# Gated mix of two attentions on one core: moved rows keep their place in the transfer queue, and two subtractions trade engines

## The chip, the core and the metric

The kernel runs on one core of a Trainium2 chip. A core has TensorE (PE) for matrix products, VectorE (DVE), ScalarE (ACT) and GpSimd (POOL) for elementwise work, and SyncE (SP), which in this kernel issues every transfer (DMA). Each engine takes its instructions in order. An instruction that waits for a semaphore holds back all that stand behind it on its engine. The metric is the device time of one execution in microseconds, the median of several runs.

## The reference

The input `x` has 2048 rows of 448 numbers. Two attentions with 16 heads of 28 numbers are computed from it and mixed by a gate:

```
g = sigmoid((x * gate_w).sum(-1))
# A, linear attention with learned softmax features
pq, pk = q @ w_phi, k @ w_phi                          # per head
phi_q  = [softmax(pq), softmax(-pq)]; phi_k likewise   # 56 features a head
num    = phi_q @ (phi_k.T @ v)
den    = phi_q @ sum_rows(phi_k) + 1e-6
a      = (num / den) @ woA
# B, softmax attention
b      = softmax(q @ k.T / sqrt(28)) @ v @ woB
out    = g * a + (1 - g) * b
```

Everything is float32. Where one float32r pass is not exact enough, an operand is split into a high part and a low part (`x - high`), and the product is made of three passes.

## The kernel before

The program is written out as one long sequence. TensorE, VectorE, ScalarE and GpSimd run their instructions in the order in which the source emits them (`manual_schedule`). SyncE is not among the engines named there: a scheduler of the framework places its transfers, as far as the data allow, and a transfer may so be put ahead of or behind another that the source wrote earlier.

There are four stages. Up to about 173 us the kernel splits `x` and the weights and makes B's queries and keys and A's key features. From 173.9 us (the first `pq`) it makes A's queries, features and outputs, up to the last `poa` at 315.2 us. Then it makes the rest of B's values, and from about 340 us (`st`, `pv`, `pm`) B's attention runs to the end. All along, scan units (`mx_unit`, tiles `pmb`, `pmd`, `rl`) look for the largest score of each query in B, as VectorE's L305 and ScalarE's L303.

The change lies in A's outputs. Here the loop over `i` (L803 and after) works on 16 blocks of 128 query rows, with two blocks to a *tile*; there are tiles 0 to 7. For each tile these steps follow one another over several turns of the loop, and the steps of neighbouring tiles interleave:

- `numer` (L560 to L572): TensorE makes numerators and denominators in `pn`, from transposed features `fT` and the key sums `KV`.
- `normalize1` (L410): ScalarE copies both halves of `pn` to `oU`. A transfer gathers the denominators, which stand in every 32nd row, into `den` (L416; `dena`, "the gather").
- `normalize2` (L419): VectorE adds a small number and takes the reciprocal (L422, L423). One transfer writes it to `rd` in memory (L426; `rda`, "the inverse"), and four read it back, spread over 32 rows each, into `rs` (L431; `rsa`, "the broadcasts").
- `normalize3` (L435): VectorE multiplies `oU` by `rs` (L437).
- `normalize4` (L440): for each of the two halves `k`, ScalarE makes the high part (L444), and VectorE or GpSimd the low part (L445), in `oT`. VectorE does it for `k == 0`, GpSimd for `k == 1`.
- `take_spread` (L453): four transfers (L457; `oTa<-oTa`, "the moved rows") copy rows of one low part into rows of `oT` that are otherwise empty, which saves TensorE one pass of twelve. They need both low parts.
- `out_a`, `out_a2` (L623 to L635): eleven passes of TensorE for each block, in `poa` (so tile n serves `poa` of blocks 2n and 2n+1); ScalarE multiplies by the gate into `ga`, and a transfer stores it in `gad` (L635, "the gated store").

`normalize1` and `normalize2` are also used by B, with `n == 1` (`denb`, `rdb`, `rsb`); A calls them with `n == 2`. Behind these transfers on SyncE's queue stand others that the text names: `qp` (L185), rows of queries for the scan units, and `vb` (L917, L918), copies of three early blocks of B's values.

Of the kernel before, what the change touches and what calls it, by code (L numbers as in the profile page):

```python
# [17 lines left out]
P = 128  # L18
# [3 lines left out]
DH = 28  # L22
# [13 lines left out]
def f32(ap):  # L36
    return ap.bitcast(F32)
# [3 lines left out]
def gated_mix_kernel(ctx, tc, xT, wqkB, wvB, wvA, wkAT, wqAT, phi, woA, woB,  # L41
# [7 lines left out]
    nc = tc.nc  # L49
# [348 lines left out]
    def fold(dst, nm, g, b0=0, n=4):  # L398
# [8 lines left out]
        nc.scalar.copy(dst[:, 0, bs, gs], pw3)  # L407
        nc.vector.tensor_sub(dst[:, 1, bs, gs], pw3, f32(dst[:, 0, bs, gs]))

    def normalize1(pool, pn, nm, n):  # L410

        oU = pool.tile([P, n, 512], F32, tag="oU", name=f"oU{nm}", bufs=1 + n)
        for i in range(n):
            (nc.scalar.copy if n == 2 else nc.vector.tensor_copy)(oU[:, i, :], pn[i])
        den = pool.tile([P, 16 * n], F32, tag="den", name=f"den{nm}", bufs=2)
        nc.sync.dma_start(den, oU[DH:P:32].rearrange("p n q -> p (n q)"))  # L416
        return oU, den

    def normalize2(pool, oU, den, nm, n, eps):  # L419

        if eps:
            nc.vector.tensor_scalar_add(den, den, EPS)  # L422
        nc.vector.reciprocal(den, den)  # L423
        rd = dr.tile([4, n * 512], F32, tag=f"rd{n}", name=f"rd{nm}", bufs=2)
        rs = pool.tile([P, n, 512], F32, tag="rs", name=f"rs{nm}", bufs=2)
        nc.sync.dma_start(rd, den)  # L426
        if n == 1:
            nc.sync.dma_start(rs[:, 0, :], rd.unsqueeze(1).to_broadcast([4, 32, 512]))
            return oU, rs
        for j in range(4):  # L430
            nc.sync.dma_start(rs[32 * j:32 * j + 32].rearrange("p n q -> p (n q)"),  # L431
                              rd[j:j + 1].to_broadcast([32, n * 512]))
        return oU, rs

    def normalize3(oU, rs, n):  # L435
# [4 lines left out]
    def normalize4(pool, oU, nm, n):  # L440

        o = pool.tile([P, n, 2, 512], F32R, tag="oT", name=f"oT{nm}", bufs=2)
        for k in range(n):
            (nc.scalar.copy if n == 2 else nc.gpsimd.tensor_copy)(o[:, k, 0, :], oU[:, k, :])  # L444
            (nc.vector if n == 2 and k == 0 else nc.gpsimd).tensor_sub(  # L445
                o[:, k, 1, :], oU[:, k, :], f32(o[:, k, 0, :]))
        if n == 2:
            spread.append(o)
        return [o[:, k] for k in range(n)]
# [3 lines left out]
    def take_spread():  # L453
        while spread:
            o = f32(spread.pop())
            for r in range(0, P, 32):
                nc.sync.dma_start(  # L457
                    o[r + DH:r + 32].rearrange("p k i n -> p (k i n)")[:, :1792].rearrange(
                        "p (s n) -> p s n", n=256),
                    o[r:r + DH, 1, 1, 256:])  # L460

    def out_passes(oT, c, w, g):
        tt = slice(c, c + P)
# [96 lines left out]
    def numer(tb):  # L560

        pn = [ps_s(f"pn{tb}_{i}") for i in range(2)]
        for gp in range(2):
            for r in range(2):
                for c in range(4):
                    n, rows = 4 * gp + c, slice(64 * r, 64 * r + 56)
                    h = 2 * n + r
                    nc.tensor.matmul(pn[r][32 * c:32 * c + 32, gp * 256:gp * 256 + 256],
                                     KV[rows, 32 * h:32 * h + 32], fT_of[tb][rows, n, :],
                                     start=True, stop=True, tile_position=(64 * r, 32 * c),  # L570
                                     skip_group_check=True)
        num[tb] = normalize1(ta, pn, f"a{tb}", 2)  # L572
# [230 lines left out]
    for i in range(2 * NT + 12):  # L803
        t, q = i, i - NT
# [65 lines left out]
        if y >= 9 and y % 2 and tb - 4 < 8:  # L870
            oTs[tb - 4] = normalize4(ta, num.pop(tb - 4), f"a{tb - 4}", 2)
            take_spread()
# [48 lines left out]
        if y >= 5 and y % 2 and tb - 2 < 8:  # L921
            num[tb - 2] = normalize2(ta, *num[tb - 2], f"a{tb - 2}", 2, True)
# [258 lines left out]
    def finish(gq, s):  # L1181
# [5 lines left out]
        def f1():  # L1187
            st["n"] = normalize1(late_p, [pv_of[gq]], f"b{gq}", 1)

        def f2():  # L1190
            st["n"] = normalize2(late_p, *st["n"], f"b{gq}", 1, False)
# [4 lines left out]
        def f4():  # L1196
            st["o"], = normalize4(late_p, st["n"], f"b{gq}", 1)
            if g < NG - 1:
                for j in range(4):
                    r = (4 * g + j) * DH  # L1200
                    nc.sync.dma_start(o_d[r:r + DH, :, qb * 512:(qb + 1) * 512],
                                      f32(st["o"][32 * j:32 * j + DH]))
# [168 lines left out]
```

## Time and profile before

| what | value |
|---|---|
| median of 3 runs | 1008.03 us (1007.89 to 1008.36) |
| profiled execution | 1007.33 us, of which the span of instructions is 1005.5 us |
| granted TensorE clock, mean | 0.997 |
| TensorE busy | 993.6 us, 99% |
| ScalarE busy | 807.4 us, 80% |
| VectorE busy | 670.0 us, 67% |
| GpSimd busy | 230.8 us, 23% |
| transfers | 109.09 MB, mean 108 GB/s |

All times inside the profile are counted from the start of the span. In a row of a timeline stand the start, the length, the engine, the line of the source, the operation, what is written and read, and how many instructions were merged; brackets give the idle time of the engine before it and what ended that. An engine with a `q` behind its name is its sequencer, which waits and issues transfers: the length of such a row is the time of issuing, not that of the transfer. The length of a matmul is modelled, so neighbouring ones overlap in the list. A wait for several semaphores is put down to the one that came last by the profile, which is not always the one that counted.

### The profile page before, as it was taken

What the parts mean: (1) busy time and instruction counts of PE and PEld (TensorE: products, weight loads), DVE (VectorE), ACT (ScalarE), POOL (GpSimd) and SP (SyncE); (2) the same over time, 40 slices, a digit from 0 to 9 for tenths busy, and PEclk for the clock granted to TensorE, in tenths of its full rate; (3) what the DMA queues carried; (4) which work ended last, traced back from release to release, by engine and by line L of the source; (5) the groups of instructions that cost most, each with busy time, mean ns of one, the idle gap of its engine ahead of it and who ended that gap; (6) DMA issues with size and microseconds to landing.
All of it is one profiled execution on the core that took longest, in us unless ns stands there. A gap on an engine that the chain in (4) does not pass through costs nothing.

```text
span 1005.5 us, 18087 instructions
## 1 busy us (share of the span) xinstructions
PE 993.6 (99%) x6456; PEld 555.5 (55%) x6456; DVE 670.0 (67%) x1343; ACT 807.4 (80%) x1532; POOL 230.8 (23%) x214
## 2 busy tenths in 40 slices
PE   9999999999989999999999999999999999999998
PEld 7878878887677533333333333333334444455656
DVE  5467666889755588888888788887886444544202
ACT  5445555568755799999999999999999999979672
POOL 1265455678414311110120101102011011101010
PEclk9999999999999999999999999999999999999999
DMA  8976312411444842332624324343233264216231
GB/s 283 318 242 212 115 62 81 165 46 54 127 147 104 168 110 50 89 78 51 130 58 107 80 52 139 82 107 92 61 85 79 52 130 114 61 37 149 63 104 56
DMA packets 69170, 109.09 MB, mean 108 GB/s; under 512 B 18216, under 2 KB 29112, under 8 KB 69080
## 3 DMA queue, kind: packets, MB, share of 16 engines
q1 hardware_dynamic: 69080, 107.94, 39.7%
q8 instruction: 51, 0.84, 0.4%
q14 instruction: 39, 0.32, 0.1%
HBM read 74.33 MB, written 31.45 MB: 105 GB/s over the span
## 4 chain that ended last, share of the span: by engine, by line
PE 95%; SPq 1%; DMA 1%; DVE 1%; ACT 0%; issue 0%; POOL 0%; POOLq 0%; ACTq 0%; DVEq 0%
PE st L1036 28%; PE pv L1140 25%; PE pm L337 9%; PE pqk L118 6%; PE pva L136 4%; PE pk L136 4%; PE pq L118 4%; PE pob L118 3%; PE pvb L136 2%; PE poa L118 2%; PE pmb L296 2%; PE pft L554 1%; PE pqk L721 1%; PE pkv L508 1%; PE poL L1178 1%; SPq L457 1%
## 5 line engine op out<-in xcount | busy, mean ns | idle before, releaser
L1039 ACT ACTIVATE p<-st 128x512 f32<-128x512 f32 x1020 | 527.8, 642 | 25.7 <-PE st L1036 25.7
L348 DVE TENSOR_REDUCE part<-pm 128x1 f32<-128x512 f32 x450 | 287.5, 685 | 150.5 <-PE pm L337 150.5
L1036 PE MATMUL st<-qst,kst 128*128 128x512 f32 x1020 | 301.1, 423 | 0.3 <-DVE acc L1155 0.3
L1140 PE MATMUL pv<-p,vb 128*32 128x512 f32 x2048 | 263.6, 602 | 0.0
L1036 PEld LDWEIGHTS st<-qst,kst 128*128 128x128 f32 x1020 | 168.7, 187 | 99.5 <-ACT p L1039 45.0
L341 ACT ACTIVATE rl<-pm 128x512 f32<-128x512 f32 x200 | 124.7, 624 | 14.0 <-PE pm L337 13.1
L337 PEld LDWEIGHTS pm<-kc,qc 28*128 28x128 f32 x800 | 38.2, 181 | 167.7 <-issue 100.6
L437 POOL TENSOR_TENSOR oUb<-oUb,rsb 128x512 f32<-128x512 f32 x15 | 19.4, 1291 | 458.2 <-DMA rsb<-rdb 293.4
L345 DVE CUSTOM_DVE_ANT_0 rl<-pm,rl 128x512 f32<-128x512 f32 x150 | 102.1, 681 | 0.0
L337 PE MATMUL pm<-kc,qc 28*128 28x512 f32 x800 | 101.1, 495 | 0.0
L1140 PEld LDWEIGHTS pv<-p,vb 128*32 128x32 f32 x2048 | 47.4, 108 | 95.6 <-issue 88.9
L305 DVE CUSTOM_DVE_ANT_0 rl<-pmb,rl 128x512 f32<-128x512 f32 x112 | 72.0, 681 | 36.8 <-ACT rl L303 36.8
L303 ACT ACTIVATE rl<-pmd 128x1024 f32<-128x1024 f32 x56 | 57.5, 1028 | 17.7 <-issue 8.7
L118 PE MATMUL pqk<-XH,wB 128*128 128x512 f32 x192 | 59.3, 397 | 0.0
L658 ACT CAST ev<-pqk 128x512 fp32r<-128x512 f32 x28 | 16.1, 588 | 38.0 <-PE pqk L118 29.7
L118 PE MATMUL poa<-woA_s,oTa 128*128 128x448 f32 x128 | 39.2, 388 | 6.5 <-DMA oTa<-oTa 3.7
L118 PEld LDWEIGHTS pqk<-XH,wB 128*128 128x128 f32 x192 | 35.4, 188 | 8.5 <-issue 1.5
L1155 DVE SCALAR_TENSOR_TENSOR acc<-pob,gate,acc 128x448 f32<-128x448 f32 x12 | 8.2, 680 | 47.2 <-PE pob L118 47.2
L136 PE MATMUL pva<-wvA_s,XH 128*128 128x450 f32 x128 | 38.6, 375 | 0.0
L659 DVE TENSOR_TENSOR ev<-pqk,ev 128x512 fp32r<-128x512 f32 x28 | 19.0, 690 | 27.8 <-ACT ev L658 27.7
L136 PE MATMUL pk<-wkA_s,XH 128*128 128x448 f32 x128 | 37.4, 373 | 0.0
L118 PE MATMUL pq<-wqA_s,XH 128*128 128x448 f32 x128 | 37.3, 374 | 0.0
(169 smaller groups left out, 1177.7 us busy)
## 6 DMA issues: line engine op xcount, KB each, us to landing
qkd<-ev SPq DMA_DIRECT2D x28, 512.0 KB
qst<-qkd SPq DMA_DIRECT2D x64, 224.0 KB
kst<-qkd SPq DMA_DIRECT2D x64, 224.0 KB
od<-oTb SPq DMA_DIRECT2D x48, 112.0 KB
rsa<-rda SPq DMA_DIRECT2D x32, 128.0 KB
rsb<-rdb SPq DMA_DIRECT2D x15, 256.0 KB
kc<-qkd SPq DMA_DIRECT2D x64, 56.0 KB
gad<-ga SPq DMA_DIRECT2D x16, 224.0 KB
```

Of the source, the lines that this page charges most:

```text
L118: nc.tensor.matmul(d, l, r, start=i == 0, stop=i == len(todo) - 1)
L136: nc.tensor.matmul(dst[:, :n], l, r, start=i == 0, stop=i == len(todo) - 1, skip_group_check=True)
L296: nc.tensor.matmul((pb if j < 2 else pd)[:, j % 2, :], qc[js, qt * P:(qt + 1) * P], kc[js, :], start=True, stop=True, tile_position=(32 * ...
L303: nc.scalar.activation(rl, pd, AF.Relu)
L305: nc.vector.tensor_tensor_reduce(rl[:, i, :], pb[:, i, :], rl[:, i, :], 1.0, LOWEST, ALU.add, ALU.max, part[:, col + i:col + i + 1])
L337: nc.tensor.matmul(pm[j], mxs[("qc", gq)][js, qt * P:(qt + 1) * P], mxs[("kc", g, kb)][js, :], start=True, stop=True, tile_position=(32 * ...
L341: nc.scalar.activation(rl, pm[kb], AF.Relu if kb < 3 else AF.Copy)
L345: nc.vector.tensor_tensor_reduce(r, pm[j], r, 1.0, LOWEST, ALU.add, ALU.max, part[:, col + j:col + j + 1])
L348: nc.vector.tensor_reduce(part[:, col + j:col + j + 1], pm[j], AX.X, ALU.max)
L1036: nc.tensor.matmul(st, kst_of[(gq // NQ, kt // 4)][:, j, (kt % 4) * P:(kt % 4 + 1) * P], qst_of[gq][:, j, :], start=True, stop=True)
L1039: nc.scalar.activation(p, st, AF.Exp, scale=SCALE)
L1140: nc.tensor.matmul(pv[32 * j:32 * j + 32, :], vb[kt // 8][:, kt % 8, 4 * g + j, :], pt[j], start=kt == 0, stop=kt == NT - 1, tile_position ...
```

## The change

The 32 transfers of moved rows, the 32 broadcasts, the 8 gathers and the 8 inverses of A get a common token. Transfers that carry one token keep the order in which the source emits them, among themselves; the scheduler still places all others. The same transfers of B (`n == 1`) get none. The gated stores get none either and stay on SyncE. In `normalize4` VectorE now makes the low part of the second half (`k == 1`) and GpSimd that of the first. No instruction is added or removed; the rows of TensorE, VectorE, ScalarE and GpSimd stand in the same order as before.

```diff
+    def kept(x, n=2):
+        if n == 2:
+            tc.stamp_issue_order_token(x.ins, "turns")
+
     def normalize1(pool, pn, nm, n):
...
-        nc.sync.dma_start(den, oU[DH:P:32].rearrange("p n q -> p (n q)"))
+        kept(nc.sync.dma_start(den, oU[DH:P:32].rearrange("p n q -> p (n q)")), n)
...
-        nc.sync.dma_start(rd, den)
+        kept(nc.sync.dma_start(rd, den), n)
...
         for j in range(4):
-            nc.sync.dma_start(rs[32 * j:32 * j + 32].rearrange("p n q -> p (n q)"),
-                              rd[j:j + 1].to_broadcast([32, n * 512]))
+            kept(nc.sync.dma_start(rs[32 * j:32 * j + 32].rearrange("p n q -> p (n q)"),
+                                   rd[j:j + 1].to_broadcast([32, n * 512])))
...
-            (nc.vector if n == 2 and k == 0 else nc.gpsimd).tensor_sub(
+            (nc.vector if n == 2 and k == 1 else nc.gpsimd).tensor_sub(
                 o[:, k, 1, :], oU[:, k, :], f32(o[:, k, 0, :]))
...
             for r in range(0, P, 32):
-                nc.sync.dma_start(
+                kept(nc.sync.dma_start(
                     o[r + DH:r + 32].rearrange("p k i n -> p (k i n)")[:, :1792].rearrange(
                         "p (s n) -> p s n", n=256),
-                    o[r:r + DH, 1, 1, 256:])
+                    o[r:r + DH, 1, 1, 256:]))
```

What this does to SyncE's queue is seen at two places. The first is around the moved rows of tiles 2 and 3. The digit behind `dena`, `rda` and `rsa` is the tile, as that behind `oTa`; the digit behind `ga` is the block. Line numbers of the changed kernel are 4 higher here. Before:

```order
L635 DMA gad0_69<-ga0_2687 128x448
L426 DMA rda3_2692<-dena3_2599 128x32
L416 DMA dena4_2749<-oUa4_2746 128x1x32
L635 DMA gad0_69<-ga1_2769 128x448
L457 DMA oTa2_2814<-oTa2_2814 4x7x256
L431 DMA rsa3_2693<-rda3_2692 32x1024 x4
L457 DMA oTa2_2814<-oTa2_2814 4x7x256 x3
L635 DMA gad0_69<-ga2_2852 128x448
L426 DMA rda4_2857<-dena4_2749 128x32
L416 DMA dena5_2917<-oUa5_2914 128x1x32
```

The same stretch of SyncE's queue in the changed kernel:

```order
L639 DMA gad0_69<-ga0_2687 128x448
L430 DMA rda3_2692<-dena3_2599 128x32
L639 DMA gad0_69<-ga1_2769 128x448
L185 DMA qp3_0_3141<-qkd_68 28x512 x2
L435 DMA rsa3_2693<-rda3_2692 32x1024 x4
L420 DMA dena4_2749<-oUa4_2746 128x1x32
L461 DMA oTa2_2814<-oTa2_2814 4x7x256 x4
L639 DMA gad0_69<-ga2_2852 128x448
L430 DMA rda4_2857<-dena4_2749 128x32
L639 DMA gad0_69<-ga3_2937 128x448
```

The broadcasts of the next tile moved from the middle of the moved rows to a place ahead of all four, the gather of the tile after it moved behind those broadcasts, and two loads of `qp` came ahead of them. The second place is the end of the stage, tiles 5 to 7, on SyncE's queue before:

```order
L416 DMA dena7_3177<-oUa7_3174 128x1x32
L635 DMA gad1_70<-ga7_3192 128x448
L457 DMA oTa5_3218<-oTa5_3218 4x7x256 x4
L635 DMA gad2_71<-ga8_3239 128x448
L426 DMA rda7_3257<-dena7_3177 128x32
L635 DMA gad2_71<-ga9_3291 128x448
L457 DMA oTa6_3304<-oTa6_3304 4x7x256
L431 DMA rsa7_3258<-rda7_3257 32x1024 x4
L457 DMA oTa6_3304<-oTa6_3304 4x7x256 x3
L635 DMA gad2_71<-ga10_3325 128x448
L917 DMA vb0_3129<-ve0_2060 128x1024
```

And the same stretch of SyncE's queue in the changed kernel:

```order
L639 DMA gad1_70<-ga7_3192 128x448
L435 DMA rsa6_3135<-rda6_3134 32x1024 x4
L420 DMA dena7_3177<-oUa7_3174 128x1x32
L461 DMA oTa5_3218<-oTa5_3218 4x7x256 x4
L639 DMA gad2_71<-ga8_3239 128x448
L430 DMA rda7_3257<-dena7_3177 128x32
L639 DMA gad2_71<-ga9_3291 128x448
L921 DMA vb0_3129<-ve0_2060 128x1024
L435 DMA rsa7_3258<-rda7_3257 32x1024 x4
L461 DMA oTa6_3304<-oTa6_3304 4x7x256 x4
L639 DMA gad2_71<-ga10_3325 128x448
```

Here the gated store of block 7 moved ahead of the broadcasts of tile 6, and the larger `vb` copy ahead of those of tile 7, which no longer part the moved rows of tile 6.

## The prediction

> **What bounds the kernel now.** I read the page's busy table and the chain that ended last first, then a table of three stretches, then the list of what TensorE waited for. In the rows of a stretch, the first pair is its length and TensorE's busy time; the granted clock stands third from the end.
>
> ```profile
> PE 993.6 (99%) x6456; PEld 555.5 (55%) x6456; DVE 670.0 (67%) x1343; ACT 807.4 (80%) x1532; POOL 230.8 (23%) x214
> ...
> PE 95%; SPq 1%; DMA 1%; DVE 1%; ACT 0%; issue 0%; POOL 0%; POOLq 0%; ACTq 0%; DVEq 0%
> ...
> 230.00:325.00 95.00, 88.53 (x581) 68.76 (x580) 63.93 (x136) 60.76 (x95) 40.18 (x33) 0.98 0.37 110
> 325.00:950.00 625.00, 624.65 (x3839) 265.52 (x3837) 435.79 (x883) 589.07 (x1173) 72.72 (x67) 1.00 0.38 89
> ...
> PE poa L118 <- DMA oTa<-oTa: 3.7, 2, 2.4
> PE poa L118 <- DMA gad<-ga: 1.9, 1, 1.9
> ...
> PE poa L118 <- ACT rl L303: 0.6, 2, 0.4
> ...
> PE poa L118 <- ACT vb L790: 0.3, 1, 0.3
> ```
>
> TensorE is the bound: 99% busy, 95% of the chain. It stands idle 11.9 us in all (1005.5 minus 993.6), and 6.5 us of that (95.00 minus 88.53) lie between 230 and 325 us, where A's output is made: the stage that the change touches. All its waits there are ahead of `poa`, the output projection of A. From 325 to 950 it waits 0.35 us in all, so an earlier start of that stretch should arrive whole at the end. The five waits by name, from TensorE's timeline, with two pieces of the chain and the clock in one of them:
>
> ```profile
> 257.02 0.64 PE L118 MATMUL poa<-woA_s,oTa 128*128 128x448 f32 x2 [0.40 <-ACT rl L303]
> ...
> 267.65 0.64 PE L118 MATMUL poa<-woA_s,oTa 128*128 128x448 f32 x2 [1.93 <-DMA gad<-ga]
> ...
> 276.99 0.65 PE L118 MATMUL poa<-woA_s,oTa 128*128 128x448 f32 x2 [0.29 <-ACT vb L790]
> ...
> 287.39 1.09 PE L118 MATMUL poa<-woA_s,oTa 128*128 128x448 f32 x2 [2.36 <-DMA oTa<-oTa]
> ...
> 310.26 0.64 PE L118 MATMUL poa<-woA_s,oTa 128*128 128x448 f32 x2 [1.31 <-DMA oTa<-oTa]
> ...
> 287.39 3.88 PE poa L118 x11
> ...
> 310.26 2.48 PE poa L118 x11
> ...
> 287.40:291.10 3.70, 3.70 (x11) 3.34 (x12) 1.70 (x3) 0.00 (x0) 1.22 (x3) 0.59 0.06 21
> ```
>
> These are the first matmuls of tiles 2, 3, 4, 5 and 7 (`oTa2` to `oTa7`). Now SyncE's own queue at the same places, which issues in order; oTa are the moved rows (L457), rsa the broadcasts (L431):
>
> ```profile
> 226.91 2.74 SPq L457 DMA_DIRECT2D oTa<-oTa  x4
> ...
> 252.18 1.98 SPq L457 DMA_DIRECT2D oTa<-oTa  x3
> ...
> 259.93 0.64 SPq L457 DMA_DIRECT2D oTa<-oTa  x1
> 260.67 2.07 SPq L431 DMA_DIRECT2D rsa<-rda  x4
> 262.78 1.98 SPq L457 DMA_DIRECT2D oTa<-oTa  x3
> ...
> 272.17 1.98 SPq L457 DMA_DIRECT2D oTa<-oTa  x3
> ...
> 281.14 0.42 SPq L635 DMA_DIRECT2D gad<-ga  x1
> 281.69 2.98 SPq L457 DMA_DIRECT2D oTa<-oTa  x4
> ...
> 304.50 2.79 SPq L457 DMA_DIRECT2D oTa<-oTa  x4
> ```
>
> From the end of the last moved row to the matmul: 254.16 to 257.02, 264.76 to 267.65, 274.15 to 276.99, 284.67 to 287.39, 307.29 to 310.26. That is 2.86, 2.89, 2.84, 2.72 and 2.97 us: one constant, the landing. So all five waits are for moved rows, also the three where the list names ScalarE or a gated store, and each ends earlier by as much as the last moved row is issued earlier. In tile 3 the first row goes at 259.93, four broadcasts of the next tile come between, and the other three follow.
>
> **The change, part by part.** *The token* puts the four moved rows together, and each tile's broadcasts ahead of them, so the broadcasts go while the queue still waits for the low parts. Unbroken, four rows take 2.74 us (tile 0). In tile 3 the span from first to last, 259.93 to 264.76, is 4.83, so 2.09 us go. Tiles 2 and 4 have the same break.
>
> - Tile 2: the 0.40 wait is smaller than that and goes: gain 0.40.
> - Tile 3: 1.93 minus 2.09, plus 0.40 by which TensorE now arrives earlier, leaves 0.24: gain 1.69.
> - Tile 4: 0.29 goes: gain 0.29. Its multiplication (L437, below) also waited 2.54 us for a broadcast that stood behind moved rows; that goes too.
> - Tile 5: its rows were not broken up, but late in the queue, and their subtractions are late:
>
> ```profile
> 277.72 1.13 ACT L444 CAST oTa<-oUa 128x512 fp32r<-128x512 f32 x2
> ...
> 278.93 1.30 POOL L445 TENSOR_TENSOR oTa<-oUa,oTa 128x512 fp32r<-128x512 f32 x1 [8.49 <-ACT oTa L444]
> ...
> 279.08 1.69 DVE L445 TENSOR_TENSOR oTa<-oUa,oTa 128x512 fp32r<-128x512 f32 x1
> ...
> 267.74 0.69 DVE L445 TENSOR_TENSOR oTa<-oUa,oTa 128x512 fp32r<-128x512 f32 x1
> ...
> 302.61 1.28 POOL L445 TENSOR_TENSOR oTa<-oUa,oTa 128x512 fp32r<-128x512 f32 x1 [13.98 <-ACT oTa L444]
> ...
> 302.71 1.73 DVE L445 TENSOR_TENSOR oTa<-oUa,oTa 128x512 fp32r<-128x512 f32 x1
> ```
>
> *The swap of the low parts.* VectorE's subtraction takes 0.69 alone (267.74) and 1.69 or 1.73 when GpSimd's runs: it ends 0.54 after GpSimd's (280.77 against 280.23), so the two go one after the other. GpSimd had the second half and waited for both casts (to 278.85). Now it has the first and may start after one cast, about half of 1.13 earlier; VectorE, busy with a scan until 279.08, still ends 0.54 behind it. So the pair ends 0.55 earlier in tiles 5 and 7. In tiles 0 to 3, where GpSimd is busy with features, I take nothing for it: its bounds there are 0 and 0.57.
>
> Tile 5 then: low parts at 280.2, and the queue is free, where it issued a store at 281.14 and the first row at 281.69. That is 1.44 earlier. TensorE arrives 0.29 earlier relative to the casts (the wait of tile 4 lies between). Wait: 2.36 plus 0.29 minus 1.44 is 1.21: gain 1.15. After this wait alone the clock fell: 0.59, and eleven matmuls took 3.88 against 2.48 after the 1.31 wait. The 1.93 wait had no such loss, so a wait of 1.21 should have none: gain 1.40. The Trainium skill ("TensorE: Matmul & The Clock Gate", Part 1) has the clock fall after an idle window of about 3.4 us. By that rule 2.36 us would not do it, the cause would be another, and the sum would be 1.40 less; the trace shows the fall right behind the gap, and I go by it.
>
> - Tile 7: GpSimd waited for both casts here too (13.98 <-ACT), and the rows went at once after VectorE (304.44 to 304.50), so only the swap counts, 0.55 to 0.60: gain 0.60 of 1.31.
>
> Sum: 0.40 + 1.69 + 0.29 + 1.15 + 1.40 + 0.60 = 5.5 us.
>
> **What is moved behind.** The gather of the next tile (`dena`, L416) now stands behind the broadcasts, and its reciprocal has a fixed place on VectorE. In tile 4 two `qp` loads stand ahead of the broadcasts, and the first waits for the scan unit's matmul at 244.39:
>
> ```profile
> 244.39 0.50 PE L296 MATMUL pmd<-kp,qp 28*128 28x512 f32 x2
> ...
> 249.74 0.12 DVE L422 TENSOR_SCALAR dena<-dena 128x32 f32<-128x32 f32 x1
> ...
> 250.99 0.62 DVE L472 TENSOR_REDUCE extq<-pcq 128x16 f32<-128x448 f32 x1 [0.74 <-ACT pcq L470]
> ...
> 265.38 1.23 DVE L437 TENSOR_TENSOR oUa<-oUa,rsa 128x1024 f32<-128x1024 f32 x1 [2.54 <-DMA rsa<-rda]
> ...
> 280.46 0.58 SPq L416 DMA_DIRECT2D dena<-oUa  x1
> ...
> 282.50 0.18 DVE L422 TENSOR_SCALAR dena<-dena 128x32 f32<-128x32 f32 x1 [1.73 <-DMA dena<-oUa]
> ...
> 274.74 2.57 DMA rda<-dena
> ...
> 250.75 1.09 PE L568 MATMUL pn<-fT,KV 56*32 56x256 f32 x32
> ...
> 259.86 1.09 PE L568 MATMUL pn<-fT,KV 56*32 56x256 f32 x32
> ```
>
> Tile 4: matmul done 244.9; two loads 0.8 (a 0.4 issue each, by `gad`'s 0.42); four broadcasts 2.07; gather 0.58; landing 1.46 (281.04 to 282.50): 249.8, against 249.74 in the place on VectorE, where 0.74 of idle follows. So it costs nothing, by a hair; from -0.5 (the 2.54 wait gone) to 0.7 for a slip are its bounds. A turn of the queue is now serial: gather 0.58, landing 1.46, reciprocal 0.5, inverse 2.57, broadcasts 2.07: 7.2 us, against 9.1 between the closest numerators (250.75 to 259.86). One half-megabyte copy (`vb`) now goes ahead of the last broadcasts; tile 6 had no wait, and I take none. The gated stores keep their engine and stand earlier or where they stood.
>
> **The rivals.**
> 1. *Part only*: tile 7 and 5 gain nothing by the swap, because the scan or the queue keeps them, and the clock still falls. Then 0.40 + 1.69 + 0.29, and 0.60 in tile 5 (1.15 less 0.55): 3.0, so 1005.0. For: VectorE's order is unchanged. Against: 8.49 and 13.98 us of idle GpSimd.
> 2. *The clock's loss stays*, its cause being something else than the gap: 5.5 minus 1.4 gives 1003.9. For: the 1.93 gap, nearly as long, had none. Against: it begins at the longest gap and nowhere else. The rule of the Trainium skill on the clock gate, above, is on this rival's side.
> 3. *The gather's turn becomes the bound*: late gathers hold VectorE at L422, and with it features and transposes. It decides once a turn exceeds 9.1 us; 7.2 plus two loads and a late store leaves about 1 us. At 2.6 over, in three tiles, it costs 7.8 against 5.5: 1010.3, slower.
> 4. *Hidden*: the waits move to another place in the stage, or the order differs without effect: 1008.0.
>
> **How the numbers follow.** The profiled execution took 1007.33 (span 1005.5 and 1.8 around it), 0.7 under the median of 1008.03. The sum gives 1001.8 against it and 1002.5 against the median, which I predict. All five waits and the clock's loss gone would be 7.7: 1000.3, the low end. 0.2%, about what can be told from no change, is 2.0 us: 1006.0, the high end, which takes in rivals 1 and 2. Chances: forecast 0.55, rival 1 0.17, rival 2 0.08, rival 3 0.11, rival 4 0.07, below the range 0.02. So faster 0.82, same 0.07, slower 0.11, and the range holds 0.80.
>
> **What would show it.** Four moved rows in one piece in every tile; waits of `poa` near 0, 0.2, 0, 1.2 and 0.7 us; clock 1.00 all through 280 to 300; GpSimd's L445 about 0.5 ahead in tiles 5 and 7; the 2.54 wait of L437 gone. I am wrong if L422 shows waits that TensorE feels, if the wait in tile 6 appears behind the `vb` copy, or if the stretch from 325 on is entered earlier and yet ends at the old time.

## The result and the profile after

The changed kernel takes 1001.9 us (median of 6 runs, 1001.0 to 1002.38), the kernel before 1007.96 (6 runs, 1007.44 to 1008.36): a ratio of 0.9939 with a 95% interval of 0.9926 to 0.9952. Forecast were 1002.5 us. The profiled execution took 1001.51 us, its span is 999.7. Line numbers are 4 higher than before. The page's busy row, two rows of the table of stretches and the list of TensorE's waits, all of the changed kernel:

```profile
PE 991.4 (99%) x6456; PEld 553.5 (55%) x6456; DVE 666.3 (67%) x1343; ACT 807.4 (81%) x1532; POOL 231.7 (23%) x214
...
230.00:325.00 95.00, 92.07 (x606) 71.26 (x606) 62.68 (x144) 62.97 (x97) 46.01 (x36) 1.00 0.44 121
325.00:950.00 625.00, 624.63 (x3840) 264.61 (x3840) 433.94 (x877) 590.48 (x1178) 66.90 (x63) 1.00 0.37 88
...
PE poa L118 <- DMA oTa<-oTa: 2.4, 3, 1.3
PE poa L118 <- ACT vb L794: 0.2, 1, 0.2
PE poa L118 <- ACT rl L303: 0.2, 1, 0.2
```

TensorE's idle time between 230 and 325 us fell from 6.5 to 2.9 us (95.00 minus 92.07), and the clock there is 1.00 instead of 0.98. From the end of the last `poa` to the end of the span it is 689.9 us before and 690.0 after, so the gain arrived whole. TensorE's timeline at the first `poa` of tiles 3, 4, 5 and 7 (tile 2 waits no more), the piece of the chain behind the longest wait, and SyncE's moved rows of tiles 2, 3, 5 and 7:

```profile
264.83 0.65 PE L118 MATMUL poa<-woA_s,oTa 128*128 128x448 f32 x2 [0.39 <-DMA oTa<-oTa]
...
274.10 0.65 PE L118 MATMUL poa<-woA_s,oTa 128*128 128x448 f32 x2 [0.22 <-ACT vb L794]
...
283.45 0.65 PE L118 MATMUL poa<-woA_s,oTa 128*128 128x448 f32 x2 [1.31 <-DMA oTa<-oTa]
...
304.40 0.64 PE L118 MATMUL poa<-woA_s,oTa 128*128 128x448 f32 x2 [0.75 <-DMA oTa<-oTa]
...
283.45 2.48 PE poa L118 x11
...
248.41 2.64 SPq L461 DMA_DIRECT2D oTa<-oTa  x4
...
259.18 2.63 SPq L461 DMA_DIRECT2D oTa<-oTa  x4
...
277.72 2.65 SPq L461 DMA_DIRECT2D oTa<-oTa  x4
...
298.66 2.68 SPq L461 DMA_DIRECT2D oTa<-oTa  x4
```

The rows go in one piece everywhere. Waits of 0, 0.39, 0.22, 1.31 and 0.75 us stand where 0.40, 1.93, 0.29, 2.36 and 1.31 stood, and the eleven matmuls after the wait in tile 5 take 2.48 instead of 3.88 us.

One part of the difference is not the change's. The spans differ by 5.8 us: 3.6 in waits of `poa`, 1.4 in the clock, and 0.9 already ahead of the first `poa` (232.73 before, 231.80 after). TensorE's timeline shows where, at the very start, of before:

```profile
1.36 3.79 PE L704 MATMUL pqk<-ident 128*128 128x128 f32 x16 [1.36 <-POOL ident masks.py:199]
5.09 3.04 PE L721 MATMUL pqk<-XH,wB 128*128 128x512 f32 x8
```

and of the changed kernel:

```profile
1.36 3.68 PE L708 MATMUL pqk<-ident 128*128 128x128 f32 x16 [1.36 <-POOL ident masks.py:199]
4.86 2.06 PE L725 MATMUL pqk<-XH,wB 128*128 128x512 f32 x8
```

The same eight matmuls took 3.04 and 2.06 us. The clock's record has its first change at 7.15 us before and at 4.80 after, and over the thirteen profiles of this study that moment lies between 4.35 and 7.57 us, and the first `poa` between 231.34 and 232.87 us, later by 0.46 us for each us. So a single profile carries up to 1.5 us of chance from its start. For the experiments I therefore also give *the stage*, the time from the first `poa` to the end of the last: 82.9 us before, 77.9 after, 5.0 less. A stage is that of one profile, and its own chance was not measured.

### The profile page after: what moved, and what is told of

The parts are those of the page before. It is cut to its first block, busy times and chain, and to the rows that moved or that the text cites. A ratio compares the mean times of both kernels' runs of the same rounds, so it can differ in the third digit from the quotient of the medians.

```text
span 999.7 us, 18087 instructions
## 1 busy us (share of the span) xinstructions
PE 991.4 (99%) x6456; PEld 553.5 (55%) x6456; DVE 666.3 (67%) x1343; ACT 807.4 (81%) x1532; POOL 231.7 (23%) x214
## 4 chain that ended last, share of the span: by engine, by line
PE 95%; DMA 2%; SPq 1%; DVE 1%; issue 1%; ACT 0%; POOL 0%; POOLq 0%; DVEq 0%; ACTq 0%
PE st L1040 28%; PE pv L1144 25%; PE pm L337 9%; PE pqk L118 6%; PE pva L136 4%; PE pk L136 4%; PE pq L118 4%; PE pob L118 3%; PE pvb L136 2%; PE poa L118 2%; PE pmb L296 2%; PE pft L558 1%; PE pqk L725 1%; PE pkv L512 1%; DMA oTa<-oTa 1%; PE poL L1182 1%
```

## The experiments

My theory at this point: TensorE waits for the moved rows, and these for the queue and the low parts; the swap is worth about 0.55 us each in tiles 5 and 7; the clock falls because the wait is long; the late gathers cost TensorE nothing.

**1. The two halves of the change apart.** The order kept, the swap undone:

```diff
-            (nc.vector if n == 2 and k == 1 else nc.gpsimd).tensor_sub(
+            (nc.vector if n == 2 and k == 0 else nc.gpsimd).tensor_sub(
```

> The order is kept as in the changed kernel, and only the swap is undone: VectorE again subtracts the first low part of a tile and GpSimd the second. My theory (the swap is worth about 0.55 us where the low parts come last, in tiles 5 and 7, and nothing in tiles 0 to 3; TensorE's clock falls only after a gap of more than 2 us): against the changed kernel TensorE's wait at poa grows by about 0.55 us in tile 5 (1.31 to about 1.85) and in tile 7 (0.75 to about 1.3), no other wait changes, TensorE stays at clock 1.00 in 280 to 300 us, time about 1003.0 us. Rival 1 (the swap gives nothing): waits as in the changed kernel, 1001.9 us. If a gap of 1.85 us is enough to lower the clock: 1.4 us more, about 1004.4 us.

Measured: 1002.37 us (5 runs; 0.9951 of before, 0.9939 to 0.9963), the stage 78.8 us, 0.9 more than with the swap. TensorE's timeline in tiles 5, 6 and 7, with GpSimd and SyncE around the `vb` copy:

```profile
284.31 0.65 PE L118 MATMUL poa<-woA_s,oTa 128*128 128x448 f32 x2 [1.43 <-DMA oTa<-oTa]
...
296.51 0.64 PE L118 MATMUL poa<-woA_s,oTa 128*128 128x448 f32 x2 [0.66 <-DMA oTa<-oTa]
...
305.80 0.64 PE L118 MATMUL poa<-woA_s,oTa 128*128 128x448 f32 x2 [0.63 <-DMA oTa<-oTa]
...
285.13 1.28 POOL L449 TENSOR_TENSOR oTa<-oUa,oTa 128x512 fp32r<-128x512 f32 x1 [7.17 <-ACT oTa L448]
286.35 0.13 POOL L920 MEMSET ve<- 128x1 f32 x2
...
286.48 0.56 SPq L921 DMA_DIRECT2D vb<-ve  x1
...
289.56 2.68 SPq L461 DMA_DIRECT2D oTa<-oTa  x4
```

The swap's worth in waits behind the first `poa` (3.55 us in all against 2.67) is 0.9 us, as in the stage, but little of it is in tile 5 (0.12) and none in tile 7 (0.63 here, 0.75 with the swap). Tile 4 has 0.18 of it (0.40 here, 0.22 with the swap), and most is in tile 6: the `vb` copy waits for a fill that stands on GpSimd behind tile 6's low part, and the broadcasts of tile 7 and the moved rows of tile 6 stand behind that copy in the queue. With the swap GpSimd begins after one cast, and the copy goes at 285.24. The 0.66 in tile 6 then shortens the wait in tile 7. My theory had the size about right (0.9 for 1.1) and the place wrong.

The copy's place in the queue is not all that it goes with. From the end of the rows' issue to the first matmul it is 4.27 us in tile 6 (289.56 plus 2.68 to 296.51), but 3.08 and 3.09 in tiles 5 and 7 of the same profile; in the three later experiments in which tile 6 waits for its rows it is 4.07 to 4.30. So the rows that stand behind the copy also land 1 us or more later than others. That the copy's 512 KB on the way make them late is likely, but was not tried apart.

The swap alone, in the order of before:

```diff
     def kept(x, n=2):
-        if n == 2:
+        if n == 9:
             tc.stamp_issue_order_token(x.ins, "turns")
```

> The swap alone, SyncE's transfers in the order of the kernel before. My theory (in tiles 3 and 5 the queue's order made the rows late, in tile 7 the low part): the wait of tile 7 falls from 1.31 to about 0.7 us, those of tile 3 (1.93) and tile 5 (2.36) stay within 0.3 us of the kernel before, the clock falls after tile 5 as before (the eleven matmuls take about 3.9 us), time about 1007.3 us. The opposite (the order does nothing, the swap does it all): tile 5's wait falls to about 1.3 us and the clock stays, time about 1002 us.

Measured: 1005.82 us (12 runs; 0.9983, 0.9973 to 0.9992). The waits of tiles 3, 5 and 7 are 2.22, 2.12 and 0.87 us and the eleven matmuls take 4.03 us: as my theory says, not as its opposite. The stage is 82.3 us, 0.6 less than before, as expected. The medians differ by 1.7 us, which is more; the nearer end of the interval is 0.8 us (the end of experiment 3 comes back to this). In the stage the order alone gives 4.1 of the 5.0 us and the swap alone 0.6, so most of the gain is the order's.

**2. Which transfers must keep their order.** Only the moved rows keep it:

```diff
-        kept(nc.sync.dma_start(den, ...), n)
+        nc.sync.dma_start(den, ...)
...
-        kept(nc.sync.dma_start(rd, den), n)
+        nc.sync.dma_start(rd, den)
...
-            kept(nc.sync.dma_start(rs[...], rd[j:j + 1]...))
+            nc.sync.dma_start(rs[...], rd[j:j + 1]...)
```

> The changed kernel with only the moved rows under the kept order; gathers, inverses and broadcasts go where they went in the kernel before. In tiles 2 to 5 and 7 the first of the four rows then stands ahead of the broadcasts of the tile two later, and the other three behind them. My theory (the broadcasts' place ahead of the rows is what the change gives): the broadcasts wait behind a row that waits for the low part, the last row goes out 2 us or more later than in the changed kernel, tile 5's wait at poa is 2.4 us or more, in most runs with a fall of the clock, time 1005 to 1008 us. Rival (only that the rows are kept in order counts): 1002 us.

Measured: 1005.68 us (10 runs; 0.9981, 0.9972 to 0.9990), as good as the swap alone, which is part of this kernel too. Tile 5 waits 2.20 us (2.4 or more was expected), the eleven matmuls after it take 4.04, and the stage is 82.3 us. SyncE's queue, from the moved rows of tile 4 to those of tile 5:

```profile
269.50 0.64 SPq L461 DMA_DIRECT2D oTa<-oTa  x1
270.24 1.78 SPq L435 DMA_DIRECT2D rsa<-rda  x4
272.06 1.98 SPq L461 DMA_DIRECT2D oTa<-oTa  x3
...
274.63 0.37 SPq L430 DMA_DIRECT2D rda<-dena  x1
...
277.31 2.37 SPq L435 DMA_DIRECT2D rsa<-rda  x4
...
281.47 2.97 SPq L461 DMA_DIRECT2D oTa<-oTa  x4
```

The time is as expected, the way there is not quite. Tile 5's rows are not split. They are late because tile 4's were: the next inverse stands behind them, then its landing, the broadcasts, and the rows of tile 5. With the full order these go at 271.42, 274.31 and 277.72, though its first `poa` is only 0.96 earlier. So the broken rows of one tile delay the next tile's whole turn. Of the three kinds of transfer set free here, the inverse stands behind the same rows in both queues, and the place of the gathers gives little (experiment 4). What the change gives is therefore the place of the broadcasts.

**3. The clock and the length of the wait.** The changed kernel with three, or six, small transfers more, right ahead of tile 5's moved rows:

```diff
+    late_rows = [0]
+    rd_x = [dr.tile([1, 512], F32, tag=f"rdx{i}", name=f"rdx{i}") for i in range(6)]
...
             o = f32(spread.pop())
+            late_rows[0] += 1
+            for i in range(3 if late_rows[0] == 6 else 0):
+                kept(nc.sync.dma_start(rd_x[i], o[i:i + 1, 0, 0, :]))
```

> The changed kernel with three more transfers of 2 KB each put on SyncE's queue right ahead of tile 5's moved rows, of data that nothing reads afterwards; the output is the same. TensorE's wait at tile 5's poa should grow from 1.31 to about 2.5 us, as long as in the kernel before, with the swap and the kept order still in place. My theory (the clock falls after a gap of that length, whatever makes it): the granted clock falls below 1.00 in 280 to 300 us and the eleven matmuls after the gap take about 3.9 us instead of 2.48, time about 1001.9 + 1.2 + 1.4 = 1004.5 us. Rival (the clock's fall in the kernel before had another cause than this gap, or needs one of 3.4 us): the matmuls take 2.48 us, about 1003.1 us.

> The same with six such transfers: the wait at tile 5's poa should grow to about 3.8 us. Both my theory and the rival that needs a gap of 3.4 us have the clock fall here: about 1001.9 + 2.5 + 1.4 = 1005.8 us. Were the clock not tied to the gap at all: 1004.4 us, the eleven matmuls at 2.48 us.

Measured with three: a wait of 2.12 us, the eleven matmuls in 3.34 us, the stage 79.8 us (1.9 more), and 1002.59 us (4 runs, in 3 of them with the fall). With six: 3.72 us, the eleven matmuls in 3.96 us, the stage 81.7 (3.8 more), and 1005.42 us (10 runs, all with the fall). A longer wait at the same place does bring the fall back, in a kernel that otherwise has none. The eleven matmuls with three take 3.34 us and not the 3.9 expected, because the fall began 1.30 us behind the first of them (283.44 and 284.74) and went on behind the last. The time with three is 1.9 us below what I expected, the stage 0.7 (1.9 more for 2.6): 0.4 because the wait grew less. The rest is not explained.

But length alone is not the rule: 2.12 us fell here and 2.22 us in tile 3 of the swap alone did not. The record of the clock gives the rest. Each fall in this stage lasts 3.41 us, and its edges lie whole multiples of 3.41 us apart from the clock's first change. The table of stretches cut at these edges, of the kernel before (the window of tile 5's wait and the next):

```profile
283.63:287.04 3.41, 1.40 (x9) 0.74 (x7) 2.96 (x8) 2.41 (x4) 0.00 (x0) 1.00 0.45 140
287.04:290.45 3.41, 3.06 (x8) 2.79 (x9) 2.06 (x3) 0.16 (x1) 1.34 (x3) 0.50 0.08 28
```

of the swap alone (the 2.22 us wait of tile 3, then tile 5):

```profile
263.22:266.63 3.41, 2.44 (x21) 1.79 (x19) 1.13 (x1) 2.58 (x5) 0.00 (x0) 1.00 0.55 176
266.63:270.04 3.41, 2.17 (x11) 1.99 (x11) 3.35 (x8) 2.17 (x5) 2.08 (x3) 1.00 0.29 88
283.69:287.10 3.41, 1.29 (x9) 0.68 (x8) 2.96 (x8) 2.57 (x4) 0.46 (x1) 1.00 0.49 158
287.10:290.51 3.41, 3.41 (x10) 3.02 (x11) 1.36 (x3) 0.00 (x0) 0.88 (x3) 0.50 0.08 29
```

of the changed kernel with three transfers more:

```profile
281.33:284.74 3.41, 1.30 (x7) 1.24 (x8) 2.96 (x6) 2.16 (x4) 1.36 (x3) 1.00 0.45 148
284.74:288.16 3.42, 3.42 (x11) 2.96 (x9) 0.15 (x1) 0.63 (x1) 0.00 (x0) 0.50 0.74 240
```

and of the changed kernel:

```profile
281.30:284.71 3.41, 2.10 (x12) 1.41 (x12) 2.95 (x8) 2.58 (x4) 0.84 (x1) 1.00 0.46 144
```

The second number is TensorE's busy time in the window, the third from the end the clock granted. A window with 1.40 us busy or less (2.01 idle or more) is followed by one at half speed; one with 2.10 us busy is not. The 2.22 us wait of tile 3 lay across an edge, 0.96 on one side and 1.26 on the other, and no fall followed. Over all windows of the thirteen profiles it holds without exception: five falls in this stage and those at the end of each run, all behind 2.01 us idle or more, and none behind 1.31 or less. Between these two it is open. The Trainium skill ("TensorE: Matmul & The Clock Gate", Part 1) calls the window 3413 ns long and free-running, and lets the clock fall after an idle one. The trace agrees on the length and on the chance of its place, but the window need not be idle: 59% sufficed.

That also fits the runs of before that were taken beside the experiments, 47 of 55 with a lowered mean clock (median 1007.55 us) and 8 without (1005.23). The 2.3 us between them are more than the 1.4 us of the one fall in the profile of before. Of the 47, 35 have a mean clock of 0.996 or 0.997, of the 12 runs of the swap alone only one has. One fall lowers the mean by 0.0017 (half of 3.41 in 1005 us), so some of the 35 may hold two falls, and the medians of experiment 1 may differ by more than the stage for this reason. No trace of these runs is kept, so this is not shown.

**4. Do the late gathers cost TensorE anything?** The gathers out of the named order:

```diff
-        kept(nc.sync.dma_start(den, oU[DH:P:32].rearrange("p n q -> p (n q)")), n)
+        nc.sync.dma_start(den, oU[DH:P:32].rearrange("p n q -> p (n q)"))
```

> The changed kernel with the gathers of the denominators left out of the named order, so that SyncE issues each gather ahead of the four broadcasts of the tile before, as in the kernel before; inverses, broadcasts, moved rows and the swap as in the changed kernel. My theory (the late gathers hold VectorE, whose waits at the guard of L426 were 1.18, 0.26, 2.80 and 1.88 us in the changed kernel, but cost TensorE little): those waits go below 0.5 us, the queue ahead of tile 5's moved rows is free 0.3 to 0.6 us earlier, tile 5's wait at poa falls from 1.31 to about 0.9 us, tile 7's stays at 0.75, time about 1001.5 us. Rival (the gathers' turn is what now sets TensorE's waits): the waits at poa fall by more than 1 us together, time about 1000.7 us or less. If the order of the gathers does not matter at all: 1001.9 us.

VectorE's timeline at the guard of the reciprocal, in the changed kernel, with the two low parts of tile 5:

```profile
249.79 0.70 DVE L426 TENSOR_SCALAR dena<-dena 128x32 f32<-128x32 f32 x1 [1.18 <-DMA dena<-oUa]
...
269.90 0.18 DVE L426 TENSOR_SCALAR dena<-dena 128x32 f32<-128x32 f32 x1 [2.80 <-DMA dena<-oUa]
...
275.60 1.30 POOL L449 TENSOR_TENSOR oTa<-oUa,oTa 128x512 fp32r<-128x512 f32 x1 [8.21 <-ACT oTa L448]
...
276.27 1.17 DVE L449 TENSOR_TENSOR oTa<-oUa,oTa 128x512 fp32r<-128x512 f32 x1
...
279.33 0.18 DVE L426 TENSOR_SCALAR dena<-dena 128x32 f32<-128x32 f32 x1 [1.88 <-DMA dena<-oUa]
```

With the gathers free these waits (and one of 0.26 at 259.70) are gone, as expected, and the time is 1001.70 us (5 runs; 0.9942, 0.9929 to 0.9956), the stage 77.6, 0.4 less. But tile 5 waits 1.39 us, not 0.9, so my theory had the waits of VectorE right and that of TensorE wrong. VectorE's low part and SyncE's rows of tile 5 in this kernel:

```profile
277.15 1.17 DVE L449 TENSOR_TENSOR oTa<-oUa,oTa 128x512 fp32r<-128x512 f32 x1
...
278.40 2.97 SPq L461 DMA_DIRECT2D oTa<-oTa  x4
```

The rows go 0.08 us after the low part (277.15 plus 1.17). With the late gather they went 0.28 after it (276.27 plus 1.17 to 277.72). The queue, until then busy with the gather, had come free just behind the low part; now the low part is the bound: two locks on one door. Counted from the first `poa`, the rows go 0.39 us earlier than in the changed kernel, but issuing them takes 0.32 us longer (2.97 for 2.65), and TensorE gets there 0.47 us earlier, in part because its wait of 0.22 in tile 4 is gone. So the wait did not become shorter, though the stage did.

**5. The other lock.** The casts and low parts ahead of the scan in the same turn, alone and with the gathers free:

```diff
-        if q in (0, 1) or q >= 11:
-            mx_unit()
         if y >= 9 and y % 2 and tb - 4 < 8:
             oTs[tb - 4] = normalize4(ta, num.pop(tb - 4), f"a{tb - 4}", 2)
             take_spread()
+        if q in (0, 1) or q >= 11:
+            mx_unit()
```

> The changed kernel with the block that casts and subtracts a tile's two parts and issues its moved rows written ahead of the call of the maximum scan in the same turn, so that on ScalarE and VectorE the casts and the low part stand ahead of the scan's copy and its two passes; SyncE's order is the same. My theory (in tile 7 the low part comes last, in tile 5 the queue, whose gather ended 0.11 us ahead of the first moved row): the low parts end 1 to 2 us earlier, tile 7's wait falls from 0.75 to about 0.1 us, tile 5's only from 1.31 to about 1.2 us, time about 1001.2 us. Rival (the low part sets both): both waits go, about 1000.0 us. If the scan, now later, holds its own reader: no gain or a loss, 1001.9 us or more.

> Both of these edits together: gathers ahead of the broadcasts, and the parts ahead of the scan. My theory (the two lie one behind the other in front of tile 5's moved rows, so that only both together free them): tile 5's wait falls to about 0.6 us or less and tile 7's to about 0.1 us, time about 1000.5 us, less than the sum of the two alone would give. Rival (the rows are held by neither): 1001.5 us or more.

Measured: 1002.93 us alone (5 runs; 0.9959, 0.9947 to 0.9972), a loss, and 1002.04 with both (5 runs; 0.9947, 0.9935 to 0.9960), no gain; the stages are 78.7 and 77.9 us. Both of my theories failed in the time. In the first it came as I had put it for a scan that holds its own reader. TensorE's waits with the parts ahead of the scan:

```profile
259.18 0.50 PE L296 MATMUL pmb<-kp,qp 28*128 28x512 f32 x2 [0.42 <-ACT rl L303]
...
260.53 0.50 PE L296 MATMUL pmd<-kp,qp 28*128 28x512 f32 x2 [0.84 <-DVE part L305]
...
269.90 0.50 PE L296 MATMUL pmd<-kp,qp 28*128 28x512 f32 x2 [0.40 <-DVE part L305]
...
284.91 0.44 PE L118 MATMUL poa<-woA_s,oTa 128*128 128x448 f32 x1 [0.40 <-DMA oTa<-oTa]
...
297.35 0.64 PE L118 MATMUL poa<-woA_s,oTa 128*128 128x448 f32 x2 [0.89 <-DMA oTa<-oTa]
```

The waits of tiles 5 and 7 fell from 2.06 to 0.40 us. In their place the scan's matmuls wait 1.66 us for their late readers, and tile 6 waits 0.89, behind the `vb` copy of experiment 1. With both edits tile 5 waits 0.37 us and tile 7 not at all, as expected, but the scan's matmuls wait 0.72 and 0.40 and tile 6 0.73. So I moved the parts for tiles 5 to 7 alone:

```diff
+        ahead = tb - 4 >= 5
-        if q in (0, 1) or q >= 11:
+        if not ahead and (q in (0, 1) or q >= 11):
             mx_unit()
...
             take_spread()
+        if ahead and (q in (0, 1) or q >= 11):
+            mx_unit()
```

> The changed kernel with the casts and low parts written ahead of the maximum scan for tiles 5, 6 and 7 only. In the kernel that did it for every tile, TensorE's waits at poa in tiles 5 and 7 fell together by 1.6 us, but 1.66 us of new waits came at the scan's own matmuls (pmb and pmd, at 259.18, 260.53 and 269.90 us, the turns of tiles 3 and 4), and 0.89 us in tile 6, whose moved rows stand in SyncE's queue behind the copy into vb. My theory (the scan's later reader costs only where the scan's matmuls follow closely, in the turns of tiles 3 and 4): those waits stay away, tile 5 waits about 0.4 to 1.2 us, tile 6 about 0.9, tile 7 about 0, time about 1001.2 us, 0.7 us below the changed kernel. If the scan is held in the later turns as well: 1002 us or more.

Measured: 1001.29 us (5 runs; 0.9940, 0.9926 to 0.9954), the stage 76.9. The scan no longer waits, nor do tiles 6 and 7, though 0.9 was expected in tile 6; tile 5 waits 1.52, above the 0.4 to 1.2 expected, since its rows stood behind the late gather: the low part ended at 276.45, the gather was issued from 276.96, and the rows went at 277.65. Next came the gathers free as well, and then the two `vb` copies one turn later too. The kernel with all three edits was run first; the expectation of the one without the later copies, which stands first here, was written after its result.

```diff
-        if q == NT + 6:
+        if q == NT + 7:
             for e in early:
                 nc.gpsimd.memset(e[:, 0, 0:1, 29:30], 0.0)
             nc.sync.dma_start(vb[0][:, 0:2], early[0])
```

> The kernel with three edits without its third: gathers ahead of the broadcasts and the parts of tiles 5 to 7 ahead of the scan, but the two copies into vb in their old place, ahead of tile 7's broadcasts and tile 6's moved rows. My theory (the copies hold tile 6's rows, which was hidden only by the wait ahead in tile 5): tile 5 waits about 0.4 us as with three edits, and a wait of 0.6 to 0.9 us appears in tile 6, where the kernel with three edits has none, time about 1000.4 us. If the copies cost TensorE nothing: no wait in tile 6, 999.7 us.

> The same with two more edits: the gathers ahead of the broadcasts, and the two copies into vb (which wait for a fill on GpSimd that stands behind tile 6's low part) one turn later, so that they no longer stand ahead of tile 7's broadcasts and tile 6's moved rows. My theory: tile 6's wait of 0.89 us goes, tile 5 waits 0.4 us, tile 7 about 0.1, all waits at poa together under 1 us, time about 1000.1 us, 1.8 us below the changed kernel. If the copies into vb are not what holds tile 6's rows, its wait stays and the time is about 1001 us; if the scan is held by the casts: 1002 us or more.

Measured: 1000.11 us without the later copies (5 runs; 0.9933, 0.9918 to 0.9949), and 999.67 with them (5 runs, 998.84 to 1000.72; 0.9928, 0.9914 to 0.9942). TensorE's waits in tiles 5 and 6 without them:

```profile
281.64 0.64 PE L118 MATMUL poa<-woA_s,oTa 128*128 128x448 f32 x2 [0.40 <-DMA oTa<-oTa]
...
293.82 0.64 PE L118 MATMUL poa<-woA_s,oTa 128*128 128x448 f32 x2 [0.62 <-DMA oTa<-oTa]
```

and with them, the two longest of all waits of `poa`, and the stretch:

```profile
264.29 0.65 PE L118 MATMUL poa<-woA_s,oTa 128*128 128x448 f32 x2 [0.40 <-ACT rl L303]
...
281.70 0.65 PE L118 MATMUL poa<-woA_s,oTa 128*128 128x448 f32 x2 [0.38 <-DMA oTa<-oTa]
...
230.00:325.00 95.00, 94.12 (x618) 72.88 (x615) 63.43 (x147) 63.84 (x99) 47.86 (x37) 1.00 0.44 122
```

Both as expected: with the copies later, the 0.62 us of tile 6 are gone. The gathers, which alone left tile 5's wait as it was (1.31 and 1.39), took 1.1 us from it (1.52 to 0.40) once the low part was out of the way. In the stage that is 0.4 us (76.9 to 76.5), because the wait in tile 6 came up in return, and 1.1 (to 75.8) with the copies later too. All five runs of the kernel with three edits are below the fastest of the changed kernel (1001.0), and its stage of 75.8 us is 2.2 less than after the change. By their times the kernels with two and with three edits cannot be told apart (999.63 to 1000.51 and 998.84 to 1000.72); the stage and the wait in tile 6 tell them apart. 0.9 us of idle time are left in the stretch.

## Why the prediction was right, point by point

- **Faster, by the moved rows' order: right.** The waits of tiles 2, 3 and 5 fell by 0.40, 1.54 and 1.05 us against 0.40, 1.69 and 1.15 forecast. The swap alone keeps those of tiles 3 and 5.
- **"All five waits are for moved rows": wrong for tile 4.** Its 0.29 was to go and 0.22 stayed. In the changed kernel its rows end 3.28 us ahead of the matmul (268.19 plus 2.63 to 274.10), longer than the landing of 2.72 to 2.97 before and than the 3.02 to 3.08 of tiles 3, 5 and 7 in the same profile. That the gap was the same length before had made it look alike. What holds it now I did not try; the list names ScalarE's `vb`.
- **The clock's 1.40 us: right in size, too simple in cause.** The wait does it, as experiment 3 shows, so rival 2 falls. But "the 1.93 wait had no such loss, so 1.21 should have none" rested on the wait's length; what counts is how much of it falls into one window.
- **The swap, 0.55 in tile 5 and 0.60 in tile 7: the sum about right (0.9 for 1.15), the places wrong.** In tile 5 the queue gave only 0.31 of the 0.5 us onward, and TensorE came earlier by 0.19. Tile 6, where I took nothing for the `vb` copy, is where it pays: without the swap that copy does hold TensorE, for 0.66 us. The wait in tile 7 fell by 0.56 after the full change, near the 0.60 forecast, but it falls as far without the swap (0.63), there because of tile 6's wait; the swap alone takes 0.44 from it.
- **The gather "costs nothing, by a hair": nearly right for TensorE (0.4 us of the stage, experiment 4), wrong for VectorE.** VectorE waits 1.18 us in tile 4's turn, and 6.1 in four turns. The sum's 249.8 was met (249.79), but by luck, since this profile runs 0.93 us earlier: VectorE was ready at 248.61 and not at 249.74. SyncE's queue shows which terms were too small:

```profile
244.00 1.33 SPq L185 DMA_DIRECT2D qp<-qkd  x2
...
247.39 0.59 SPq L420 DMA_DIRECT2D dena<-oUa  x1
```

Loads and broadcasts took 3.39 us (244.00 to 247.39), not 2.87 (0.8 and 2.07), and from the gather's issue to its result it was 2.40, not 2.04 (0.58 and 1.46). The limit of rival 3 did not hold either: from one gather to the next it was 9.72, 10.39 and 9.53 us (247.39, 257.11, 267.50 and 277.03), more than 9.1, yet no matmul of `pn` waited and the rival's loss did not come. In tile 5 the price was small because the rows went only 0.28 us after the low part.

- **The sum, 5.5 us against 6.1 by the medians.** In the stage it was 5.0, 0.5 less than the working gave, and by the medians 0.6 more. The start of the runs, and perhaps a second fall in runs of before, lie in the medians and in no term of the sum. That 1002.5 came so near to 1001.9 is therefore in part luck.

## What to carry to other kernels

A stall that one wait ends can have two causes one close behind the other; taking away one shows little, and the price of each is only known with the other gone (the late gathers: freeing them left tile 5's wait as it was, and took 1.1 us from it once the low part came earlier). In a shared transfer queue ask of every transfer what stands behind it: a copy that nobody needs yet held rows that TensorE waited for, and broken rows of one tile made the next tile late. Ahead of a comparison of two single profiles, subtract what differs before the changed place.

## What the hardware showed unexpectedly

- The clock is decided in windows of 3.41 us. TensorE idle for 2.01 us or more of one means half speed in the next; 1.31 us does not, nor did a wait of 2.22 us that lay across an edge. Of 3.41 us at half speed 1.4 to 1.6 us were lost where the fall began ahead of the eleven matmuls (3.88 to 4.04 us for 2.48).
- The same windows set the start: the clock rises for the first time between 4.35 and 7.57 us, and the first `poa` moves by 0.46 us for each us of that. Between the thirteen profiles that makes up to 1.5 us (231.34 to 232.87).
- Where VectorE's and GpSimd's subtractions overlap, VectorE's ends 0.54 us behind GpSimd's whichever has which half: in the changed kernel 277.44 and 276.90 in tile 5, before 280.77 and 280.23. Alone it takes 0.69, so it looks as if the two went one after the other.
- Moved rows that stood behind a copy of 512 KB in the same queue landed 1 us or more later than others (4.07 to 4.30 us from the end of their issue to the matmul that waited, against 2.7 to 3.1 in tiles 3, 5 and 7 of all profiles).
